# A fused attention and two-layer kernel: the first layer's gate as a tanh, a padding tile in its own pool, and a re-ordered list of steps for the first stage

## Chip, core and metric

The kernel runs on one core of a Trainium2 chip. The metric is the device time of one execution in microseconds; the profiled execution is one such run, recorded instruction by instruction. The engines are named as in the profile: PE is the matrix engine (PEld its weight loads), DVE the vector engine, ACT the scalar engine, POOL the GpSimd engine, and SP issues the transfers.

## What is computed

Three parts follow each other: attention with a feature map for 4 batches of 8 heads (576 positions, head size 64), a gated layer pair of 512 to 2048 to 512 for 2304 tokens, and a sum over four experts of 512 to 1024 to 512.

```python
def phi(x):
    proj = np.einsum('bhsd,df->bhsf', x, w_phi)
    proj = proj - np.max(np.abs(proj), axis=-1, keepdims=True)
    return np.concatenate([np.exp(proj), np.exp(-proj)], axis=-1)
...
num = np.einsum('bhsf,bhfd->bhsd', q_p, np.einsum('bhsf,bhsd->bhfd', k_p, v))
den = np.einsum('bhsf,bhf->bhs', q_p, np.sum(k_p, axis=2))[..., None] + 1e-06
...
h = x @ w_in
g = h * (1.0 / (1.0 + np.exp(-1.702 * h)))
x = g @ w_out
...
for e in range(E):
    h = np.maximum(x @ w1[e], 0.0)
    out += p[:, e:e + 1] * (h @ w2[e])
```

The weights `w_in` and `w_out` arrive as 64-bit floats, the rest as 32-bit floats.

## The kernel before, in words

The tokens are cut in two groups of 1024 and 1280, and each layer's hidden width in units of two 128-wide blocks: units 0 to 7 are the first layer on the first group, 8 to 15 the same layer on the second group, 16 to 47 the experts. A product of 32-bit values is made of three passes over a rounded high part (copied by ACT) and a low part (a subtraction, L208, on POOL or DVE).

The first stage holds the attention of 16 pairs of heads and, woven into it, units 0 to 6 of the first layer. There every step is a word of one long list, `ORDER`, and `in_order` ties each instruction to the one before it on its engine, so that the list fixes the order on PE, DVE, ACT, POOL and SP. A word such as `3.kn0` is a step of head pair 3; `q`, `k`, `v`, `n`, `t` are its matrix products, `kn`, `kp`, `en`, `ep` the exponentials of keys and queries (L591, L594, L549, L552). `h5.abs` and its like turn half a block of 64-bit weights into 32 bits: `abs` (L286), `rb` (L288) and `sg` (L290) on ACT, `cl` and `sh` (L292, L294) on DVE or POOL, `ad` and `mu` after them. In words of the layer, `F` is the first product (`plain_first`, L790), `Va` the sigmoid (L909), `Vb` its product with the hidden value (L912), `Ha` and `Hb` the high and low part, `S` the second product (`plain_second`, L825) and `E` its addition into `xa` (L834).

Unit 7 comes after the list, in `plain_unit`, with the second products of unit 6 between its own, and the preparation of unit 8 (`prep_sums`, `prep_in`, and the operands `xo` that `build_x` makes by subtractions on DVE, L389) goes beside it as background. From unit 8 on every unit is a `strassen_unit` of seven products per quarter (L733), and the second products of the unit before stand between them.

Before the first transfer lands, PE runs seven products of a zero tile (`warm`, L203). `norm_probs` (L434 to L437) scales the expert weights on DVE; it is outside the list, and the compiler places it.

Of the kernel before, what the change touches and what calls it, by code (L numbers as in the profile page):

```python
# [18 lines left out]
P = 128  # L19
# [23 lines left out]
EDGE = 120  # L43
NU = 7
# [28 lines left out]
h2.cl:1 0.v1 0.ve@0 2.k1@n5 1.ldv 2.k0@w1 1.rd1 h3.ld 2.qx1@1 2.qm0@1 3.ldk@1 3.qe1 1.kn0 0.ep 0.n0@w0 0.n1 4.ldq@1
5.ldq@0 2.kx1@0 2.ks1@0 2.kx0@0 1.kp1 1.rd2 2.qm1 1.kp0 2.ks0@0 2.r@n4 2.rm@0 2.ldv h2.sg 1.v0@n5 h2.sh 2.rd1 3.qx1@0
h3.abs 2.kn0 h3.sg 0.n2 0.fa@0 5.q0@w1 5.qx0@1 h2.rb@1 1.v1 1.ve@1 2.kp0 2.kn1 3.qm1 3.k0@w3 2.kp1 3.r@n4 1.es:0 1.en
2.v0@n5 0.fr 5.qe0@0 3.kx0@1 h2.ad:1 0.fm@0 4.ldk@0 3.rm@1 5.q1@w0 5.qe1 wl0.0:0 5.qm0@1 3.k1@n4 3.kx1@1 2.v1 1.ep
0.t1@w1 0.t0 2.ve@0 h3.rb@0 0.fh:0 3.ks0@1 2.rd2 3.kn0 3.ldv h2.mu:0 3.rd1 5.qx1@0 3.ks1@1 3.kp0 2.es:0 5.qm1 h3.cl:1
h4.ld h4.abs 4.q1@w3 4.k1@n5 4.q0@w0 4.qx0@1 4.qx1@0 1.n0@w1 1.n1 1.n2 h4.cl:1 4.qm0@0 4.qm1 4.kx1@0 5.ldk@1 5.k1@n4
5.kx1@1 8.ldq@0 4.qe0@2 4.qe1 1.fa@1 5.ks1@0 3.rd2 3.kn1 3.kp1 3.es:0 5.k0@w0 1.fr 5.r@n6 2.en 2.ep 4.ldv 5.kn1 h3.sh
5.rm@0 6.ldq@1 4.r@n7 4.rm@1 6.ldk@1 3.v0@n4 3.v1 3.ve@1 5.kx0@0 5.ks0@0 4.rd1 4.rd2 4.k0@w3 4.kx0@1 3.en 3.ep 2.n0@w0  # L80
2.n1 h4.rb@1 4.ks1@1 4.kn1 4.kp1 5.kn0 1.fm@1 4.ks0@1 4.kn0 5.rd1 2.n2 1.t1@w2 6.q0@w1 2.fa@0 6.qx0@1 1.t0 3.n0@w3
3.n1 1.fh:1 6.qe0@3 2.fr 2.fm@0 3.n2 3.fa@1 5.ldv 4.kp0 5.kp1 6.q1@w2 6.qx1@0 7.ldk@0 6.k0@w1 h3.ad:1 h3.mu:0 wl0.1:0
5.kp0 7.ldq@1 h5.ld 4.es:0 4.v0@n0 4.v1 xh0 xl0:0 5.rd2 6.kx0@0 6.qe1 3.fr 3.fm@1 4.en 4.ep 4.ve@0 h5.abs 5.v0@n1 5.v1
6.qm0@1 6.ks0@1 6.kn0 6.kp0 h5.sg 6.qm1 6.k1@n6 6.kx1@1 6.ks1@1 3.t1@w2 6.r@n7 6.rm@1 3.t0 3.fh:1 2.t1@w1 7.k1@n0 2.t0
2.fh:1 7.k0@w3 6.kn1 6.kp1 5.es:0 4.n0@w2 h4.sh 5.en 7.kx0@1 h4.ad:1 5.ep 6.ldv 4.n1 5.ve@1 4.n2 h5.cl:1 6.v0@n2 6.rd1
4.fa@0 7.kx1@0 6.v1 h4.sg 6.ve@0 8.ldk h4.mu:0 4.fr 4.fm@1 xh3 7.ks1@0 7.kn1 7.q1@w2 7.ks0@0 4.t1@w0 4.t0 4.fh:0
7.q0@w1 7.qx1@1 7.qx0@0 7.qm0@0 7.qm1 7.qe0@1 6.rd2 7.qe1 5.n0@w3 5.n1 5.n2 xl3:0 h5.rb@0 8.q0@w0 8.qe0@0 8.q1@w1 st0
7.r@n4 h5.sh 8.qe1 7.rm@0 h6.ld h6.abs 6.es:0 5.fa@1 5.fr 6.en 6.ep 5.fm@0 h6.sg 7.rd1 7.rd2 h5.ad:0 h5.mu:1 h6.cl:1
h7.ld h7.sg wi1 wl1.0:0 F0.0.0@n5 Va0.0.0@0 5.t1@w3 5.t0 5.fh:1 F0.1.0@n4 7.kp1 8.qx0@0 8.k1@n6 8.qx1@1 8.qm0@1 8.qm1
# [61 lines left out]
def fused(ctx: ExitStack, tc: tile.TileContext, qT, kT, v, w_phi, wg1, wg2, probs, out):  # L151
# [855 lines left out]
    def plain_unit(unit):  # L1007
        for n, (i, k, tag, behind) in enumerate(PLAIN):
# [5 lines left out]
            if n:  # L1014
                build_next()
# [78 lines left out]
```

## Time and profile before

| what | value |
|---|---|
| runs | 1333.04, 1338.75, 1336.97 us, median 1336.97 |
| profiled execution | 1336.96 us, span of its records 1335.2 us |
| PE busy | 1304.4 us, 98% of the span |
| DVE, POOL, ACT busy | 774.8, 679.8, 571.9 us (58%, 51%, 43%) |
| first product of unit 8 starts at | 345.41 us |

Busy is the time in which an engine had an instruction at work. PE is busy nearly always, so the table alone says little: what matters is in which stretches PE waits, for whom, and at which granted clock it works. [...]

### The profile page before, as it was taken

The page shows a single profiled execution, that of the slowest core. Times are in us where ns is not written, and L with a number is a line of the kernel's source. Part 1 is how long each engine was busy: PE and PEld are TensorE (multiplying, and loading weights), DVE is VectorE, ACT ScalarE, POOL GpSimd, SP SyncE. Part 2 cuts the span into 40 slices and gives each one's busy share as a digit, 9 for nine tenths or more (in the row PEclk, how much of TensorE's full clock was granted, in tenths as well). Part 3 has the DMA queues.
Part 4 walks back from the last instruction along what each step waited for, and adds up shares of the span by engine and source line. Part 5 has one row for each costly group of instructions (what it writes and reads, how often), then busy time and mean ns, then how long its engine had stood idle before and what let it go on. Part 6 is the DMA issues. An engine that isn't in the chain of part 4 may idle for free.

```text
span 1335.2 us, 19948 instructions
## 1 busy us (share of the span) xinstructions
PE 1304.4 (98%) x8231; PEld 1068.7 (80%) x8231; DVE 774.8 (58%) x1111; ACT 571.9 (43%) x824; POOL 679.8 (51%) x480
## 2 busy tenths in 40 slices
PE   7999999988999999999999999899999999999998
PEld 5877777777788888888888888778888888888887
DVE  7877768767834447654545545775455445445445
ACT  6889888775453334523323223243223222222310
POOL 4774656446956656855354463537324423443320
PEclk8999999989999999999999999999999999999999
DMA  7654434441100101011011110113001100110102
GB/s 219 202 169 142 149 122 158 143 146 64 64 32 32 63 33 32 32 64 64 32 64 61 34 64 32 63 32 127 32 32 36 60 32 32 56 40 32 32 0 79
DMA packets 45708, 96.87 MB, mean 73 GB/s; under 512 B 22706, under 2 KB 22834, under 8 KB 43570
## 3 DMA queue, kind: packets, MB, share of 16 engines
q1 hardware_dynamic: 45618, 95.61, 22.1%
q8 instruction: 64, 1.05, 0.3%
q14 instruction: 26, 0.21, 0.1%
HBM read 82.42 MB, written 13.18 MB: 72 GB/s over the span
## 4 chain that ended last, share of the span: by engine, by line
PE 88%; DVE 5%; ACT 4%; issue 1%; DMA 1%; POOL 0%; SPq 0%; DVEq 0%; ACTq 0%; POOLq 0%
PE psa L864 29%; PE psa L733 28%; PE psa L862 8%; PE psa L790 5%; PE psa L813 5%; PE psa L825 5%; PE psa L624 2%; PE psa L606 2%; DMA raws<-in_wg_dram 1%; PE psa L561 1%; PE psa L500 1%; ACT L909 1%; DVE xt L389 1%; PE psa L599 1%; DVE raws L389 1%
## 5 line engine op out<-in xcount | busy, mean ns | idle before, releaser
L733 PE MATMUL psa<-xo,win 128*128 128x512 f32 x1680 | 426.2, 392 | 1.0 <-DVE hs L740 0.9
L864 PE MATMUL psa<-wout,g 128*128 128x512 f32 x1536 | 387.8, 394 | 3.5 <-DVE xa L884 3.5
L733 PEld LDWEIGHTS psa<-xo,win 128*128 128x128 f32 x1680 | 315.0, 188 | 71.7 <-DVE hs L740 1.3
L864 PEld LDWEIGHTS psa<-wout,g 128*128 128x128 f32 x1536 | 286.8, 188 | 68.0 <-DVE xa L884 3.9
L208 POOL TENSOR_TENSOR wout<-raw,wout 128x1024 fp32r<-128x1024 f32 (+1 forms) x53 | 116.6, 2203 | 386.5 <-ACT wout L335 377.2
L884 DVE SCALAR_TENSOR_TENSOR xa<-psa,pn,xa 128x512 f32<-128x512 f32 x198 | 148.4, 749 | 144.2 <-PE psa L864 143.7
L711 ACT ACTIVATE g<-psa 128x512 fp32r<-128x512 f32 x96 | 57.5, 599 | 395.8 <-DVE psa L740 276.4
L208 POOL TENSOR_TENSOR g<-sg,g 128x512 fp32r<-128x512 f32 x59 | 79.4, 1350 | 93.8 <-ACT g L707 60.3
L712 DVE SCALAR_TENSOR_TENSOR g<-psa,g 128x512 fp32r<-128x512 f32 x96 | 66.4, 691 | 94.3 <-ACT g L711 94.3
L208 POOL TENSOR_TENSOR win<-raw,win 128x1024 fp32r<-128x1024 f32 (+1 forms) x51 | 113.9, 2236 | 11.0 <-ACT win L349 11.0
L208 POOL TENSOR_TENSOR win<-ss,win 128x1024 fp32r<-128x1024 f32 x40 | 98.0, 2450 | 9.5 <-ACT win L327 9.4
L825 PE MATMUL psa<-g,wout 128*128 128x512 f32 x384 | 99.0, 401 | 2.7 <-POOL g L208 0.7
L790 PE MATMUL psa<-xo,win 128*128 128x512 f32 x384 | 96.3, 400 | 2.8 <-DVE xa L834 2.1
L862 PE MATMUL psa<-g,wout 128*128 128x512 f32 x384 | 96.7, 394 | 0.0
L740 DVE TENSOR_TENSOR uu<-psa,mm 128x512 f32<-128x512 f32 x80 | 55.2, 690 | 64.0 <-PE psa L733 64.0
L825 PEld LDWEIGHTS psa<-g,wout 128*128 128x128 f32 x384 | 69.8, 188 | 22.4 <-issue 2.1
L790 PEld LDWEIGHTS psa<-xo,win 128*128 128x128 f32 x384 | 71.0, 190 | 20.5 <-DVE xa L834 2.9
L862 PEld LDWEIGHTS psa<-g,wout 128*128 128x128 f32 x384 | 71.2, 188 | 15.4
L813 PEld LDWEIGHTS psa<-xr,win 128*128 128x128 f32 x576 | 75.2, 189 | 4.0
L813 PE MATMUL psa<-xr,win 128*128 128x256 f32 x576 | 76.2, 281 | 0.0
L316 POOL TENSOR_TENSOR ss<-raw 128x256 f32<-128x256 f32 x80 | 61.9, 774 | 14.3 <-DMA raw<-in_wg_dram 9.0
L876 DVE TENSOR_TENSOR xa<-psa,xa 128x512 f32<-128x512 f32 x49 | 33.7, 689 | 35.2 <-PE psa L862 35.1
(126 smaller groups left out, 1700.9 us busy)
## 6 DMA issues: line engine op xcount, KB each, us to landing
raw<-in_wg_dram SPq DMA_DIRECT2D x32, 1024.0 KB
raws<-in_wg_dram SPq DMA_DIRECT2D x32, 512.0 KB
w_d<-raw SPq DMA_DIRECT2D x8, 1024.0 KB
raw<-w_d SPq DMA_DIRECT2D x8, 1024.0 KB
qraw<-in_qT_dram SPq DMA_DIRECT2D x16, 288.0 KB
kraw<-in_kT_dram SPq DMA_DIRECT2D x16, 288.0 KB
xa<-mx_d SPq DMA_DIRECT2D x8, 576.0 KB
mb<-mx_d SPq DMA_DIRECT2D x8, 576.0 KB
```

What stands on the lines that cost most here:

```text
L208: eng.tensor_tensor(out=dst, in0=src, in1=hi.bitcast(F32), op=ALU.subtract)
L316: nc.gpsimd.tensor_tensor(out=ss[:, n], in0=x0, in1=x1, op=op)
L711: nc.scalar.activation(out=hi, in_=src, func=AF.Relu)
L712: nc.vector.scalar_tensor_tensor(out=lo, in0=src, scalar=0.0, in1=hi.bitcast(F32), op0=ALU.max, op1=ALU.subtract)
L733: nc.tensor.matmul(ps, win[self.u][:, a, w, kc * P:(kc + 1) * P], xo[i][:, e, kc, :], start=start and k_ == 0, stop=stop and k_ == 5, skip ...
L740: nc.vector.tensor_tensor(out=out, in0=ps, in1=other, op=ALU.add)
L790: nc.tensor.matmul(ps, win[self.u][:, a, 2 * i + kc // 2, (kc % 2) * P:(kc % 2 + 1) * P], x[:, e, kc % 2, :], start=(n == 0), stop=(n == 11),)
L813: nc.tensor.matmul(ps, win[self.u][:, a, 2 * i + kc // 2, (kc % 2) * P:(kc % 2 + 1) * P], xo["rest"][e][:, kc, :], start=(k_ == 0), stop=( ...
L825: nc.tensor.matmul(ps, wout[self.u][:, a, i, t * P:(t + 1) * P], self.g[i, k][:, e, :], start=(n == 0), stop=(n == 5))
L862: nc.tensor.matmul(p, w[:, a, i, t_ * P:(t_ + 1) * P], v_, **f)
L864: nc.tensor.matmul(p, v_[:, t_ * P:(t_ + 1) * P], w[:, a, i, :], **f)
L884: nc.vector.scalar_tensor_tensor(out=o, in0=ps, scalar=col, in1=o, op0=ALU.mult, op1=ALU.add)
```

## The change

The gate h·sigmoid(1.702h) is computed as h·(1 + tanh(0.851h)), which is twice as large, and the conversion of `w_out` from 64 bits makes it half as large by other constants in the same two instructions. The padding tile `edge` is allocated in a pool of its own. The list is a new one: it now holds unit 7 and the preparation of unit 8 too (words `D`, `ld`, `ss`, `pi`, `px`), and one step `w3` with three more products of the zero tile; `plain_unit` and `PLAIN` are gone.

```diff
-NU = 7
+NU = 8
...
 ORDER = """
-0.ldq@0 0.q1@w0 h1.ld h1.abs h1.rb@0 0.qx1@0 0.ldk@0 h0.ld h0.abs 1.ldq@1 0.q0@w1 0.qx0@1 0.qm0@0 0.qm1 h1.cl:1
+0.ldq@0 0.q0@w0 0.qx0@0 0.q1@w1 0.qx1@1 h0.ld h0.abs h0.sg 1.ldq@1 w3@n6 1.q0@w2 h1.ld 1.q1@w3 0.qe0@0 0.qm0@0 0.qm1
...
+    edge = ctx.enter_context(tc.tile_pool(name="edge", bufs=1, side="right"))
+    edge.tile([P, EDGE], F32, name="edge")
     right = ctx.enter_context(tc.tile_pool(name="right", bufs=1, side="right"))
-    right.tile([P, EDGE], F32, name="edge")
...
         elif k == "rb":
-            nc.scalar.activation(out=rb[s], in_=l.bitcast(U32), func=AF.Copy, scale=2.0 ** -51, bias=2.0)
+            nc.scalar.activation(
+                out=rb[s], in_=l.bitcast(U32), func=AF.Copy, scale=2.0 ** (-51 - q // 2), bias=2.0 - q // 2
+            )
...
-            eng.tensor_scalar(out=m, in0=m, scalar1=W_MIN, scalar2=W_MAX, op0=ALU.max, op1=ALU.min)
+            eng.tensor_scalar(
+                out=m, in0=m, scalar1=W_MIN * (1 + q // 2 / 8), scalar2=W_MAX, op0=ALU.max, op1=ALU.min
+            )
...
+    def gate(out, src):
+
+        nc.scalar.activation(out=out, in_=src, func=AF.Tanh, scale=0.851)
+
+    def gated(t, src):
+        nc.vector.scalar_tensor_tensor(out=t, in0=t, scalar=1.0, in1=src, op0=ALU.add, op1=ALU.mult)
...
-                nc.scalar.activation(out=sg, in_=src, func=AF.Sigmoid, scale=1.702)
-                nc.vector.tensor_tensor(out=sg, in0=src, in1=sg, op=ALU.mult)
+                gate(sg, src)
+                gated(sg, src)
...
-                nc.scalar.activation(out=unit.sg[i, j], in_=src, func=AF.Sigmoid, scale=1.702)
+                gate(unit.sg[i, j], src)
...
-                nc.vector.tensor_tensor(out=sg, in0=src, in1=sg, op=ALU.mult)
+                gated(sg, src)
...
+        if name[0] == "w" and name[1].isdigit():
+            warm(int(name[1:]), int(slot[1:]))
...
+        elif name == "D":
+            third_area()
+        elif name[:2] in made:
+            next(made[name[:2]])
+        elif name[:2] == "px":
+            next(bx["023".index(name[2])])
...
-        (plain_unit if plain(u) else strassen_unit)(unit)
+        strassen_unit(unit)
```

How the new list moves instructions is shown at three places. The first is ACT, early in the stage, where the first gates of the layer stand between the exponentials of head pairs (`ek` of keys, `eq` of queries). ACT_TABLE_LOAD brings in the table of a function. Before:

```order
L349 CAST win_1073<-raw_134 128x1024
L909 ACT_TABLE_LOAD
L909 ACTIVATE sg_95<-psa 128x512
L594 ACT_TABLE_LOAD
L594 ACTIVATE ek_111<-ek_111 128x128
L349 CAST wout_89<-raw_133 128x1024
L909 ACT_TABLE_LOAD
L909 ACTIVATE sg_96<-psa 128x512
L591 ACT_TABLE_LOAD
L591 ACTIVATE ek_110<-ek_110 128x1024
L365 CAST xo_1187<-xa_71 128x1024
L594 ACTIVATE ek_110<-ek_110 128x1024
```

The same place in the new list, where L701 is the tanh and L593, L596, L551, L554 the exponentials:

```order
L593 ACTIVATE ek_113<-ek_113 128x1024
L514 COPY eq_111<-psa 128x2x288
L284 ACTIVATE raw_137<-raws_1_88 128x512
L596 ACTIVATE ek_113<-ek_113 128x1024
L701 ACTIVATE sg_98<-psa 128x512
L286 ACTIVATE xt_89<-raws_0_87 128x512
L286 ACTIVATE xt_90<-raws_1_88 128x512
L551 ACTIVATE eq_112<-eq_112 128x1152
L701 ACTIVATE sg_99<-psa 128x512
L919 CAST g_93<-sg_98 128x512
L554 ACTIVATE eq_112<-eq_112 128x1152
L671 COPY xa_74<-psa 128x448
```

No load stands between gates and exponentials any more; the built program has 42 loads on ACT before and one, its first instruction, now. The second place is DVE at the start, from the first large key subtraction (`ek` from psa and `mx`) of pair 0 on. Before:

```order
L586 TENSOR_TENSOR ek_110<-psa,mx_118 128x1024
L521 TENSOR_REDUCE r_115<-mb_107 128x2x9 x2
L518 STREAM_TRANSPOSE mb_107<-psa 128x576
L434 TENSOR_REDUCE psum_p<-pn 128x18
L435 TENSOR_SCALAR psum_p<-psum_p 128x18
L436 RECIPROCAL psum_p<-psum_p 128x18
L437 TENSOR_TENSOR pn<-pn,psum_p 128x72
L531 TENSOR_REDUCE m_117<-psa 36x32
L518 STREAM_TRANSPOSE mb_107<-psa 128x576
```

And now:

```order
L588 TENSOR_TENSOR ek_113<-psa,mx_121 128x1024
L520 STREAM_TRANSPOSE mb_110<-psa 128x576
L581 TENSOR_REDUCE mx_123<-psa 128x1
L533 TENSOR_REDUCE m_120<-psa 36x32
L588 TENSOR_TENSOR ek_114<-psa,mx_123 128x128
L581 TENSOR_REDUCE mx_124<-psa 128x1
L523 TENSOR_REDUCE r_117<-mb_110 128x2x9
L588 TENSOR_TENSOR ek_134<-psa,mx_124 128x128
L520 STREAM_TRANSPOSE mb_110<-psa 128x576 x2
```

The four instructions of `norm_probs` have left this place; they stand some 40 rows later. The third place is DVE at the end of the stage, where the subtractions of `build_x` (into `xt` and `raws`) are made. Before:

```order
L834 TENSOR_TENSOR xa_71<-psa,xa_71 128x512
L389 TENSOR_TENSOR xt_87<-xa_72 128x512 x2
L389 TENSOR_TENSOR xt_86<-xt_87,xa_72 128x512 x2
L389 TENSOR_TENSOR raws_0_84<-xa_72,xt_86 128x512 x2
L389 TENSOR_TENSOR raws_1_85<-xa_72 128x512
L834 TENSOR_TENSOR xa_71<-psa,xa_71 128x512 x2
L389 TENSOR_TENSOR raws_1_85<-xa_72 128x512
L834 TENSOR_TENSOR xa_71<-psa,xa_71 128x512 x2
```

And now, where L391 are the subtractions, L838 the additions into `xa`, L704 the gate's product and L300 a step of a weight's conversion:

```order
L391 TENSOR_TENSOR xt_90<-xa_75 128x512 x2
L300 SCALAR_TENSOR_TENSOR raw_137<-raws_0_87,raw_137 128x512
L704 SCALAR_TENSOR_TENSOR sg_98<-sg_98,psa 128x512
L704 SCALAR_TENSOR_TENSOR sg_99<-sg_99,psa 128x512
L838 TENSOR_TENSOR xa_74<-psa,xa_74 128x512
L391 TENSOR_TENSOR xt_89<-xt_90,xa_75 128x512 x2
L391 TENSOR_TENSOR raws_0_87<-xa_75,xt_89 128x512 x2
L838 TENSOR_TENSOR xa_74<-psa,xa_74 128x512 x3
```

The eight subtractions, seven of them in one piece before, are now broken into pieces of two, four and two, with gates and additions between.

## Rows read from the trace of the kernel before

**Rows 1.** The page: span and busy times of PE and PEld.

```profile
span 1335.2 us, 19948 instructions
...
PE 1304.4 (98%) x8231; PEld 1068.7 (80%) x8231; DVE 774.8 (58%) x1111; ACT 571.9 (43%) x824; POOL 679.8 (51%) x480
```

**Rows 2.** Stretches: length, then busy time by engine, granted PE clock, DMA share, GB/s.

```profile
0.00:345.40 345.40, 323.73 (x3623) 255.50 (x3624) 258.88 (x385) 272.72 (x381) 207.30 (x147) 0.97 0.48 149
0.00:40.00 40.00, 30.86 (x413) 22.18 (x415) 30.20 (x49) 26.28 (x41) 22.45 (x29) 0.91 0.73 213
40.00:345.40 305.40, 292.86 (x3218) 233.31 (x3213) 228.68 (x337) 246.44 (x341) 184.85 (x119) 0.98 0.44 141
```

**Rows 3.** Shorter stretches of the same view, where the granted clock was half.

```profile
13.80:20.70 6.90, 5.63 (x21) 2.39 (x21) 6.80 (x10) 5.46 (x10) 6.74 (x5) 0.51 0.77 243
...
92.40:95.70 3.30, 3.30 (x60) 3.30 (x62) 3.17 (x5) 3.11 (x4) 2.83 (x3) 0.50 0.02 3
...
181.10:184.40 3.30, 3.30 (x52) 3.18 (x48) 0.45 (x2) 1.25 (x3) 2.57 (x2) 0.50 0.36 114
...
293.80:300.50 6.70, 5.91 (x76) 5.47 (x77) 3.64 (x8) 5.12 (x8) 1.30 (x1) 0.50 0.51 151
```

**Rows 4.** Groups by line: the first and last of six groups of table loads.

```profile
L909 ACT ACT_TABLE_LOAD x21 | 26.9, 1283 | 2.5 <-PE psa L790 2.2
...
L286 ACT ACT_TABLE_LOAD x1 | 1.3, 1283 | 0.7 <-PEq L1080 0.7
```

**Rows 5.** Timeline of PE: its three longest waits after 40 us, in brackets.

```profile
92.28 1.97 PE L606 MATMUL psa<-v,ek 128*64 128x65 f32 x32 [1.80 <-ACT ek L594]
...
180.15 2.95 PE L624 MATMUL psa<-kv,eq 128*64 128x65 f32 x64 [2.31 <-ACT eq L552]
...
294.60 4.17 PE L624 MATMUL psa<-kv,eq 128*64 128x65 f32 x72 [3.13 <-ACT kv L613]
```

**Rows 6.** Timeline of ACT ahead of those three waits.

```profile
87.98 1.28 ACT L591 ACT_TABLE_LOAD   x1
...
91.17 1.05 ACT L594 ACTIVATE ek<-ek 128x1024 f32<-128x1024 f32 x1
...
177.64 1.28 ACT L552 ACT_TABLE_LOAD   x1
...
291.82 1.28 ACT L552 ACT_TABLE_LOAD   x1
```

**Rows 7.** Timeline of PE at the end of the stage.

```profile
319.92 0.73 PE L825 MATMUL psa<-g,wout 128*128 128x512 f32 x2 [0.71 <-ACT g L915]
321.38 2.56 PE L825 MATMUL psa<-g,wout 128*128 128x512 f32 x10 [0.73 <-POOL g L208]
326.04 5.76 PE L790 MATMUL psa<-xo,win 128*128 128x512 f32 x24 [2.10 <-DVE xa L834]
...
345.41 1.54 PE L733 MATMUL psa<-xo,win 128*128 128x512 f32 x6
```

**Rows 8.** Timeline of DVE at the end of the stage.

```profile
317.46 2.74 DVE L389 TENSOR_TENSOR xt<-xa 128x512 f32<-128x512 f32 x2
...
325.31 1.28 DVE L834 TENSOR_TENSOR xa<-psa,xa 128x512 f32<-128x512 f32 x2
```

**Rows 9.** Timeline of DVE and PE in the start.

```profile
18.95 2.30 DVE L437 TENSOR_TENSOR pn<-pn,psum_p 128x72 f32<-128x72 f32 x1
...
22.20 1.16 PE L561 MATMUL psa<-w_st,kraw 64*128 64x128 f32 x16 [1.49 <-DVE mb L518]
```

**Rows 10.** Groups by line: a fused DVE instruction, the gate's two, zero products.

```profile
L712 DVE SCALAR_TENSOR_TENSOR g<-psa,g 128x512 fp32r<-128x512 f32 x96 | 66.4, 691 | 94.3 <-ACT g L711 94.3
...
L912 DVE TENSOR_TENSOR sg<-psa,sg 128x512 f32<-128x512 f32 x28 | 19.2, 686 | 19.7 <-ACT sg L909 19.5
...
L909 ACT ACTIVATE sg<-psa 128x512 f32<-128x512 f32 x28 | 16.8, 598 | 6.2 <-PE psa L790 4.1 <-DVE g L208 1.6 <-POOL g L208 0.3
...
L203 PE MATMUL psa<-zero 128*128 128x512 f32 x7 | 3.4, 652 | 1.4 <-DVE zero L199 1.4
```

More of the change, by code (lines that the diff above doesn't have):

```diff
@@ L73 @@
[L73 to L77, printed above, removed]
@@ L147 @@
+S6.0.0@n7 E6.0.0 px2.1 ol7.1:0 E6.1.2 Ha7.0.1@2 Hb7.0.1:1 F7.1.1@n6 S6.0.3@n4 pi8.2 pi8.3 Va7.1.1@0 Vb7.1.1 Ha7.1.1@1
+px2.2 px3.1 ah1.0 ah1.1 px3.2 E6.0.3 Hb7.1.1:0 ld9 E6.1.0
 """
@@ L199, in fused, with warm @@
     nc.vector.memset(zero[:, 0, 0, :].bitcast(F32), 0.0)
-    def warm(n):
+    def warm(n, b=0):
         for _ in range(n):
-            nc.tensor.matmul(bank(0), zero[:, 0, 0, 0:P], zero[:, 0, 0, :], start=True, stop=True)
+            nc.tensor.matmul(bank(b), zero[:, 0, 0, 0:P], zero[:, 0, 0, :], start=True, stop=True)
     warm(WARM)
@@ L794, in plain_first @@
                     n += 1
-        def plain_value(self, i, k, ps):
-            older, self.stages = self.stages, deque()
-            self.value(i, k, ps)
-            self.finish(older)
         def finish(self, stages):
@@ L920, in fused @@
     pairs = [Pair(i) for i in range(B * NP)]
-    ready = build_x(1)
+    bx = build_x(1)
+    made = {"ss": prep_sums(NU), "pi": prep_in(NU)}
     def step(word):
@@ L938, in step @@
             pump(pre)
+        elif name == "D":
[4 more added lines that the diff above has]
+            next(bx["023".index(name[2])])
+        elif name[:2] == "ld":
+            next(load(int(name[2:])))
         elif name[:2] in ("xh", "xl"):
@@ L954, in fused @@
         in_order(lambda: step(word))
-    third_area()
+    for _ in range(3):
+        bx.popleft()
     norm_probs()
@@ L958, in fused @@
     ring["g"] = deque([g for g in gs if not any(g is x for x in held)] + held)
-    bg.append(load(NU + 1))
     before = units[NU - 1]
@@ L1005, in build_next @@
             free.append(bx.popleft())
-    def plain_unit(unit):
-        for n, (i, k, tag, behind) in enumerate(PLAIN):
-            ps = bank(TAGS.index(tag))
-            unit.plain_first(i, k, ps)
-            background(1)
-            seconds(*behind, paced=True)
-            unit.plain_value(i, k, ps)
-            if n:
-                build_next()
     def strassen_unit(unit):
@@ L1032, in fused @@
             bx = ready
-        if u + 1 < len(UNITS) and not plain(u + 1):
+        if u + 1 < len(UNITS):
             bg.append(prep_sums(u + 1))
```

161 lines of the change are left out of this document (81 added, 80 removed).

## Prediction

> **What bounds the kernel now.** I read the page first. PE is busy for 1304.4 of 1335.2 us [rows 1], so a gain can only come from time in which PE waits or works slowly. Next I read the view by stretches. The first stage, up to the first product of unit 8 at 345.41 us, has 323.73 us of busy PE [rows 2, 7], so 345.40 − 323.73 = 21.7 us of the kernel's 30.8 us of idle PE lie in it. Of these, 40.00 − 30.86 = 9.1 us fall into the first 40 us and 305.40 − 292.86 = 12.5 us into the rest [rows 2]. The reader should see here that ACT, the second busiest engine of the stage, is at work for 272.72 us of 345.40, and for 246.44 us of the 305.40 us after the start [rows 2]: 81% against 75% on DVE.
>
> The granted clock adds a second loss. [...] The last three follow the three longest waits of PE after the start: it waited 1.80 us up to 92.28, 2.31 us up to 180.15 and 3.13 us up to 294.60 [rows 5], and the clock was at 0.50 from 92.4, 181.1 and 293.8 on [rows 3].
>
> The view of the waits says who ended these three: an exponential of keys, one of queries, and the copy `kv` that stands behind one of queries [rows 5]. ACT's own timeline shows table loads in front of each: the loads at 87.98, 177.64 and 291.82 us are the last of four, four and three within the 13 us before, at 1.28 us each [rows 6]. So it is a queue on ACT, and not the data, that was late there.
>
> **The change part by part.** *Table loads.* Before, there are 42 loads, in six groups of which the largest is the 21 ahead of the sigmoid, at 1283 ns each [rows 4]. In the new program ACT has one. ACT is given back 41 × 1.283 = 52.6 us, so that 272.72 − 52.6 = 220 us are left in the stage. What of this reaches PE is read from the waits: in front of each of the three, the loads sum to 5.1, 5.1 and 3.8 us, more than the wait itself. I take all three waits off: 1.80 + 2.31 + 3.13 = **7.24 us**. The bounds are 0, if the same exponentials are late for another reason, and 7.24. Most other loads lie beside work of PE and are worth nothing; their cover is the products that PE has queued, and where a new order has less queued, one load would have cost at most its 1.28 us.
>
> *Clock.* In the three stretches PE was busy for 3.30 + 3.30 + 5.91 = 12.51 us at half speed [rows 3]. The same work at full speed is half of it: **6.25 us** back, provided that the waits go. Bounds: 0 and 6.25.
>
> *The end of the stage.* PE waits 0.71, 0.73 and 2.10 us there [rows 7]; the last was ended by an addition into `xa` that stood on DVE behind seven subtractions of `build_x`, one piece from 317.46 to 325.31 us [rows 8]. The new list breaks that piece up and puts gates and additions between. I take the three waits off: **3.54 us**, with 0 as the other bound. What is late next there is the operand `xo` of unit 8: the same subtractions end later when they yield to the gates, and they had some 20 us of PE's products as cover before (326.04 to 345.41). If that cover is short, PE waits at the first products of unit 8.
>
> *The start.* `norm_probs` held DVE for 2.30 us with its last instruction, and a transpose behind it ended a 1.49 us wait of PE [rows 9]. The four instructions now stand after the first pairs. I take **1.5 us**. Bounds: 0, and 9.1 + 2.8 = 11.9 us if all idle time of the start went, 5.63 / 2 = 2.8 us of which is the slow clock from 13.8 to 20.7 [rows 2, 3]; I take the low end since the first transfers and the chain from them to the first exponentials stay. Three more zero products cost about 3.4 / 7 = 0.5 us each, 1.5 us together [rows 10]. They stand between the queries of pair 0 and those of pair 1, where PE has no other work before DVE's and ACT's answers; I cost them at nothing, and at 1.5 us without that cover.
>
> *The gate itself.* No row shows a tanh. The sigmoid of 128x512 took 598 ns [rows 10], and ACT's instructions of that shape are within some tens of ns of it whatever they compute; I take the same. The fused instruction on DVE, 691 ns where it reads the matrix result beside an on-chip tile, stands against 686 ns for the plain product [rows 10]: 80 of them come to 80 × 5 ns = 0.4 us, off the path. The factor of one half rides on immediates of instructions that were there already, and the tile `edge` is never written or read: nothing.
>
> *What the new order adds.* The list changes the place of nearly every instruction of the stage, so new waits are sure to come. Their bounds are 0 and several of the kind seen. I take one of 2.10 us, like the longest that let the clock stand [rows 7].
>
> **Sum.** 7.24 + 6.25 + 3.54 + 1.5 − 2.1 = 16.4 us. The profiled execution took 1336.96 us, against a median of 1336.97, so the forecast for the median is 1336.96 − 16.4 = **1320.5 us**. Everything from unit 8 on keeps its order and its durations. A limit from above: after the start the stage can give back at most 12.5 + 6.25 = 18.8 us, so most of the forecast is that the stage becomes nearly free of waits.
>
> **The rivals.** *The waits stay, only their cause is renamed.* ACT had 73 us of idle time in the stage even with the loads, so an exponential may be late because DVE's maximum or a transfer was late. For this speaks that the largest of the three was a copy of `kv`, two instructions behind the exponential; against it, that ACT ran without a gap ahead of the first two. Only the end and the start would then gain, 3.54 + 1.5 = 5.0 us: 1332 us.
>
> *Slower.* In the new list PE waits for an engine that its order has put too late, and each such wait is paid twice, by itself and by the clock after it. By the middle one of the three this is 2.31 + 3.30 / 2 = 4.0 us. The place would be the change from unit 7 to unit 8, where DVE must finish the subtractions, low parts and additions in the time of PE's last products, or the first pairs, where the order is quite another one. Five such waits eat up 18.5 us of gains; to be slower by 0.5% takes 25.2 / 4.0, so more than six, and it gives 1343 us or more. Three in 300 us is what the trace of before shows, with ACT far fuller.
>
> *The clock holds through the start too.* It fell at 13.8 us after a stretch in which PE had little to do, and was back at 20.7 us [rows 3]. Three more zero products just ahead of that place could keep it up: 2.8 us more, 1317.7 us. [...] I leave this out of the likeliest sum.
>
> *More than the sum.* The stage loses all waits after 40 us and half of the start's 11.9 us: 18.8 + 6 = 24.8 us, 1312 us.
>
> **How the numbers follow.** The measurement of this kernel can tell about 0.5%, 6.7 us, from no change: faster means below 1330.3 us, slower above 1343.6 us. I give the forecast with its terms 0.50, the clock through the start 0.17, more than the sum 0.18, the renamed waits 0.10, and the slower list 0.05. The first three are faster, 0.85; the renamed waits are the same, 0.10. The range reaches down to 1310 us, which is the last gain with 2 us to spare, and up to 1331 us, which is the forecast with the 3.54 and the 1.5 us lost and about 5 us more of new waits; I leave out about 0.07 below and 0.12 above.
>
> **What would show it.** In the profile of the changed kernel ACT should have one table load, and ACT's busy time up to the first product of unit 8 should be near 220 us. That product should start near 329 us instead of 345.41. The clock should not be at half speed after 40 us, and no wait of PE for an exponential should exceed 1 us. The addition into `xa` should end no wait at the end of the stage, and the first products of unit 8 should follow without a wait for `xo` or for low parts of unit 7's weights. From unit 8 on, stretches should have their old lengths. The forecast is wrong if a wait of 2 us or more stands in the new stage with a fall of the clock behind it, if DVE, now the fullest engine after PE, ends such waits, or if the start takes longer since its key products come later.

## The result and the profile after

The changed kernel takes 1313.97 us (median of 4 runs, 1312.72 to 1314.64) beside 1336.65 us for the kernel before: a ratio of 0.9832 [0.9809, 0.9855], 22.7 us less. The forecast was 16.4 us less. The sign came as written, and the first stage to within 2.5 us, but two amounts that the sum does not contain, one in each direction, are as large as its biggest terms. The page of the changed kernel, beside [rows 1]:

```profile
span 1312.2 us, 19912 instructions
PE 1283.3 (98%) x8234; PEld 1070.4 (82%) x8234; DVE 780.5 (59%) x1117; ACT 516.7 (39%) x784; POOL 672.9 (51%) x472
```

Table loads in the view of groups, beside [rows 4]: one is left of 42, and it is the first instruction of ACT.

```profile
L284 ACT ACT_TABLE_LOAD x1 | 1.3, 1283 | 0.7 <-PEq L1085 0.7
```

The view by stretches, with the columns of [rows 2]; the granted clock is a share of full speed. The first product of unit 8 (L742, the L733 of before) starts at 326.53 us; unit 8 ends where unit 9's first product starts, at 360.39 us.

```profile
0.00:326.53 326.53, 313.45 (x3627) 255.89 (x3627) 256.18 (x383) 216.42 (x339) 191.87 (x135) 0.98 0.49 155
0.00:40.00 40.00, 34.78 (x529) 26.33 (x531) 31.92 (x54) 29.08 (x46) 20.30 (x26) 1.00 0.77 226
40.00:326.53 286.53, 278.67 (x3100) 229.56 (x3100) 224.25 (x329) 187.34 (x294) 171.57 (x109) 0.98 0.45 145
326.53:360.39 33.86, 26.80 (x115) 20.78 (x114) 31.27 (x34) 13.81 (x21) 30.15 (x19) 0.90 0.18 62
360.39:1312.20 951.81, 943.03 (x4495) 793.69 (x4493) 493.09 (x701) 286.44 (x425) 450.89 (x320) 1.00 0.13 46
```

The last two stretches of the kernel before, in the same view:

```profile
345.41:370.63 25.22, 24.48 (x115) 19.68 (x114) 21.70 (x26) 12.51 (x19) 21.28 (x14) 1.00 0.13 43
370.63:1335.20 964.57, 956.23 (x4495) 793.53 (x4493) 494.16 (x701) 286.62 (x425) 451.27 (x320) 1.00 0.14 46
```

Read as three parts, the 23.0 us between the profiled spans are −18.88 up to unit 8, +8.64 in unit 8, and −12.76 from unit 9 on. The last part is the surprise: the same 4495 products, with idle time of 8.78 us against 8.34, and yet PE's busy time is 13.2 us less. PE does not wait less there. About 1 us of the 12.76 lies in unit 30, where the second group of tokens of the experts is prepared: the clock was at half there for 6.8 us in the kernel before and for 3.4 us in the changed one. The view by stretches, before and then after:

```profile
849.13:876.14 27.01, 23.53 (x91) 18.64 (x90) 21.27 (x23) 5.85 (x8) 12.48 (x7) 0.87 0.12 39
832.71:858.73 26.02, 22.30 (x91) 18.00 (x90) 21.19 (x23) 5.84 (x8) 12.59 (x7) 0.93 0.12 41
```

In the other units the products themselves follow each other more closely: in the experts' first group the second products of odd units start 227 ns apart in the median, where they had 234 (table below). Unit 8 is the opposite: 7.06 us of idle PE where there were 0.74, and a granted clock of 0.90.

The waits of PE between 40 us and unit 8, by what was waited for: us in total, times, longest.

```profile
PE psa L563 <- DVE ek L588: 3.0, 1, 3.0
PE psa L569 <- DMA kraw<-in_kT_dram: 2.3, 1, 2.3
PE psa L658 <- DVE on L641: 2.1, 2, 1.9
```

The three waits behind ACT of [rows 5] are gone. Three others have come: for DVE up to 46.87 us, for DVE again up to 100.31 and for a transfer up to 183.17. The view by stretches has half a clock behind each, as in [rows 3]:

```profile
46.80:50.20 3.40, 3.33 (x38) 3.10 (x40) 3.23 (x6) 2.80 (x5) 1.37 (x1) 0.51 0.38 83
101.40:104.80 3.40, 3.40 (x70) 3.40 (x66) 0.62 (x2) 2.77 (x5) 0.31 (x1) 0.50 0.53 148
183.30:186.70 3.40, 3.40 (x12) 2.03 (x13) 1.55 (x4) 1.94 (x5) 2.79 (x2) 0.50 0.03 5
```

**Unit 8.** PE's timeline at the change of units, beside [rows 7] (L742 are unit 8's first products, L829 second products of unit 7):

```profile
326.53 1.07 PE L742 MATMUL psa<-xo,win 128*128 128x512 f32 x4
327.92 0.73 PE L742 MATMUL psa<-xo,win 128*128 128x512 f32 x2 [0.33 <-DVE xo L206]
332.96 4.37 PE L829 MATMUL psa<-g,wout 128*128 128x512 f32 x10 [4.30 <-DVE sg L704]
338.72 1.63 PE L742 MATMUL psa<-xo,win 128*128 128x512 f32 x6 [1.39 <-DVE xa L838]
```

The 4.30 us were ended by a gate's product on DVE (L704), because that product is the last reader of the accumulation bank that PE wants next. DVE's timeline shows what stood ahead of it; L206 is the low part of a split, L391 the subtractions of `build_x`, L838 the additions:

```profile
328.39 1.17 DVE L206 TENSOR_TENSOR xo<-xt,xo 128x512 fp32r<-128x512 f32 x1
329.48 0.68 DVE L838 TENSOR_TENSOR xa<-psa,xa 128x512 f32<-128x512 f32 x1
330.08 2.23 DVE L206 TENSOR_TENSOR g<-sg,g 128x512 fp32r<-128x512 f32 x1
332.23 0.67 DVE L704 SCALAR_TENSOR_TENSOR sg<-sg,psa 128x512 f32<-128x512 f32 x1
332.83 1.15 DVE L206 TENSOR_TENSOR xo<-xt,xo 128x512 fp32r<-128x512 f32 x1
333.91 3.47 DVE L391 TENSOR_TENSOR raws<-xa 128x512 f32<-128x512 f32 x2
337.30 1.87 DVE L838 TENSOR_TENSOR xa<-psa,xa 128x512 f32<-128x512 f32 x3
```

DVE has no gap here, and its instructions of one shape differ widely: an addition that reads one operand from the matrix result takes 0.68 us, while a subtraction of two on-chip tiles takes 1.15, 1.17 or 2.23 us. POOL's timeline beside it:

```profile
328.97 2.79 POOL L206 TENSOR_TENSOR win<-ss,win 128x1024 fp32r<-128x1024 f32 x1
331.72 3.41 POOL L206 TENSOR_TENSOR xo<-xa,xo 128x512 fp32r<-128x512 f32 x2
```

The 2.23 us instruction started at 330.08, inside POOL's instruction, which ended at 331.76, and ended 0.55 us after it. Over the whole changed kernel such instructions on two on-chip tiles took 1.22 us in the median where a POOL instruction overlapped them and 0.68 us where none did (numbers in the last section), and the additions from the matrix result 0.68 us in both cases. So in this trace the ones held up stand beside POOL; why, no run shows. PE's granted clock then stood at 0.50 from 330.1 to 336.9 us.

### The profile page after: what moved, and what is told of

It reads as the page before. It is cut to its first block, busy times and chain, and to the rows that moved or that the text cites. A ratio compares the mean times of both kernels' runs of the same rounds, so it can differ in the third digit from the quotient of the medians.

```text
span 1312.2 us, 19912 instructions
## 1 busy us (share of the span) xinstructions
PE 1283.3 (98%) x8234; PEld 1070.4 (82%) x8234; DVE 780.5 (59%) x1117; ACT 516.7 (39%) x784; POOL 672.9 (51%) x472
## 4 chain that ended last, share of the span: by engine, by line
PE 89%; DVE 6%; DMA 3%; POOL 1%; issue 1%; ACT 0%; SPq 0%; DVEq 0%; ACTq 0%
PE psa L868 29%; PE psa L742 28%; PE psa L866 8%; PE psa L829 6%; PE psa L799 6%; PE psa L817 5%; PE psa L626 2%; PE psa L608 1%; DMA xa<-mx_d 1%; DVE xo L206 1%; PE psa L502 1%; PE psa L563 1%; POOL eq L548 1%; DVE raws L391 1%; DMA kraw<-in_kT_dram 1%
## 5 line engine op out<-in xcount | busy, mean ns | idle before, releaser
L742 PE MATMUL psa<-xo,win 128*128 128x512 f32 x1680 | 421.5, 390 | 3.0 <-DVE xa L838 1.4
L868 PE MATMUL psa<-wout,g 128*128 128x512 f32 x1536 | 381.3, 391 | 3.7 <-DVE xa L888 3.7
L742 PEld LDWEIGHTS psa<-xo,win 128*128 128x128 f32 x1680 | 314.4, 188 | 69.3 <-ACT win L329 1.8
L206 POOL TENSOR_TENSOR wout<-raw,wout 128x1024 fp32r<-128x1024 f32 (+1 forms) x51 | 113.9, 2235 | 372.6 <-ACT wout L337 369.5
L206 POOL TENSOR_TENSOR g<-sg,g 128x512 fp32r<-128x512 f32 x56 | 77.3, 1381 | 96.2 <-ACT g L716 59.3
L206 POOL TENSOR_TENSOR win<-raw,win 128x1024 fp32r<-128x1024 f32 (+1 forms) x52 | 115.5, 2224 | 5.6 <-ACT win L351 3.0
L206 POOL TENSOR_TENSOR win<-ss,win 128x1024 fp32r<-128x1024 f32 x40 | 98.3, 2457 | 8.3 <-ACT win L329 8.2
L829 PE MATMUL psa<-g,wout 128*128 128x512 f32 x384 | 96.7, 401 | 5.2 <-DVE sg L704 4.3
L866 PE MATMUL psa<-g,wout 128*128 128x512 f32 x384 | 95.3, 390 | 0.0
L799 PE MATMUL psa<-xo,win 128*128 128x512 f32 x384 | 92.4, 392 | 0.4 <-POOL win L206 0.2
L829 PEld LDWEIGHTS psa<-g,wout 128*128 128x128 f32 x384 | 73.1, 193 | 23.3 <-DVE sg L704 4.7
L799 PEld LDWEIGHTS psa<-xo,win 128*128 128x128 f32 x384 | 71.5, 188 | 17.2 <-POOL win L206 0.7
L866 PEld LDWEIGHTS psa<-g,wout 128*128 128x128 f32 x384 | 71.1, 188 | 14.4 <-DVE xa L880 0.2
L701 ACT ACTIVATE sg<-psa 128x512 f32<-128x512 f32 (+1 forms) x72 | 39.3, 548 | 84.8 <-DVE psa L749 32.5
```

The source lines that it names most:

```text
L206: eng.tensor_tensor(out=dst, in0=src, in1=hi.bitcast(F32), op=ALU.subtract)
L742: nc.tensor.matmul(ps, win[self.u][:, a, w, kc * P:(kc + 1) * P], xo[i][:, e, kc, :], start=start and k_ == 0, stop=stop and k_ == 5, skip ...
L799: nc.tensor.matmul(ps, win[self.u][:, a, 2 * i + kc // 2, (kc % 2) * P:(kc % 2 + 1) * P], x[:, e, kc % 2, :], start=(n == 0), stop=(n == 11),)
L829: nc.tensor.matmul(ps, wout[self.u][:, a, i, t * P:(t + 1) * P], self.g[i, k][:, e, :], start=(n == 0), stop=(n == 5))
L866: nc.tensor.matmul(p, w[:, a, i, t_ * P:(t_ + 1) * P], v_, **f)
L868: nc.tensor.matmul(p, v_[:, t_ * P:(t_ + 1) * P], w[:, a, i, :], **f)
```

## The experiments

All times are set beside runs of the kernel before on the same chip (medians 1334.0 to 1337.9 us). "First" is the start of unit 8's first product in the profile, "unit 8" its length. The moved addresses of the later experiments and the kernel without the filler were executed once each; their unit lengths and the spacing of their products tell more than their times.

### What each part is worth

**The gate alone**: the kernel before, its old list and old padding, with the tanh and the halved `w_out`. One of the two places of the gate; the constants of the conversion are those of the change:

```diff
-                nc.scalar.activation(out=sg, in_=src, func=AF.Sigmoid, scale=1.702)
-                nc.vector.tensor_tensor(out=sg, in0=src, in1=sg, op=ALU.mult)
+                nc.scalar.activation(out=sg, in_=src, func=AF.Tanh, scale=0.851)
+                nc.vector.scalar_tensor_tensor(out=sg, in0=sg, scalar=1.0, in1=src, op0=ALU.add, op1=ALU.mult)
```

> The kernel before (old list, padding in the common pool) with only the tanh gate and the halved w_out: one table load. By the prediction's first two terms the three waits of 1.80, 2.31 and 3.13 us and the slow clock behind them go, 13.5 us: about 1323 us. Rival, that those exponentials were late for another reason or that the old list puts its waits elsewhere: 1333 to 1337 us.

Measured: 1319.67 us (1317.61 to 1321.45), ratio 0.9877 [0.9861, 0.9894]. First at 328.56 us, 16.85 earlier than before; unit 8 25.17 us, as before. All that is left of PE's waits between 40 us and unit 8, in the view of waits:

```profile
PE psa L825 <- POOL g L208: 1.1, 1, 1.1
PE psa L790 <- DVE xa L834: 0.9, 1, 0.9
PE psa L825 <- ACT g L915: 0.7, 1, 0.7
```

The clock is at full speed from 40 us to unit 8, beside the third line of [rows 2]:

```profile
40.00:328.56 288.56, 285.82 (x3227) 228.40 (x3223) 225.09 (x337) 192.51 (x300) 184.62 (x119) 1.00 0.47 149
```

The tanh takes as long as the sigmoid did, 596 against 598 ns [rows 10]. So the loads caused the three long waits and the slow clock behind them, the last three of the four stretches of [rows 3], in the old order. The gain is some 3 us more than expected.

**The loads back**: the changed kernel, with its new list and pool, and the sigmoid and the whole `w_out` again (42 loads).

```diff
-        nc.scalar.activation(out=out, in_=src, func=AF.Tanh, scale=0.851)
+        nc.scalar.activation(out=out, in_=src, func=AF.Sigmoid, scale=1.702)
```

> The changed kernel (new list, padding in its own pool) with the sigmoid and the full w_out again, so that ACT has its 42 table loads. If the loads are what the stage gained by, its waits for exponentials come back: 10 to 16 us more than the changed kernel, 1324 to 1330 us. Rival, that the new order would hide them: 1314 to 1317 us.

Measured: 1332.91 us (1326.48 to 1336.28), ratio 0.9971 [0.9954, 0.9989]. First at 345.71, unit 8 34.93 us. The waits for ACT are back, in other places:

```profile
PE psa L626 <- ACT eq L554: 6.4, 2, 5.2
PE psa L563 <- DVE ek L588: 3.7, 1, 3.7
PE psa L626 <- ACT xa L671: 3.0, 1, 3.0
```

The loads cost 18.9 us under the new list (1332.91 − 1313.97), some 3 us more than the expectation's upper end, and 17.2 and 14.6 under the old one (without and with the padding moved; medians against the kernel before and against the padding alone, below). The rival of the renamed waits falls on both sides.

**The padding alone**: the kernel before with two lines moved.

```diff
+    edge = ctx.enter_context(tc.tile_pool(name="edge", bufs=1, side="right"))
+    edge.tile([P, EDGE], F32, name="edge")
     right = ctx.enter_context(tc.tile_pool(name="right", bufs=1, side="right"))
-    right.tile([P, EDGE], F32, name="edge")
```

> The kernel before with only the padding tile in its own pool; nothing else differs. Addresses: this moves the tiles wout0, g0 to g4 and sg0, sg1 by 480 bytes, from an address of 96 modulo 128 to one of 0 modulo 128. Theory A, the address of these operands sets the pace of the products: from unit 9 on the units take 26.24, 20.40 and 26.04 us as in the changed kernel, 12 us in sum, and the first stage gains about 2 us by its 720 products, so about 1322.5 us. Theory B, the quicker later units come from the gate or the list: no change, 1336.7 us.

Measured: 1323.83 us (1320.52 to 1326.97), ratio 0.9904 [0.9882, 0.9926]. First at 347.21 us, no earlier than before; unit 8 25.13; the units behind it have exactly the lengths of the changed kernel: 26.24 us (before 26.33 and 26.58 in turn), 20.40 (20.67 and 20.84), 26.04 (26.32 and 26.42). From unit 9 on, beside the second of the two stretches of the kernel before above:

```profile
372.34:1325.20 952.86, 944.06 (x4495) 794.40 (x4493) 493.22 (x701) 286.56 (x425) 450.91 (x320) 1.00 0.14 46
```

That is 11.7 us less than before, with unit 30 at 27.05 us as before. In this profile the first stage did not gain the 2 us that were expected of it.

**All but the padding**: the changed kernel with the tile back in `right`.

> The changed kernel with the padding tile back in the pool of the other tiles. Theory A: units from 9 on as slow as before (26.33 and 26.58, 20.67 and 20.84, 26.32 and 26.42 us), 12 us, and the first stage about 2 us longer: about 1328 us. Theory B: 1314 us.

Measured: 1325.04 us (1322.42 to 1326.55), ratio 0.9911 [0.9896, 0.9926]. First at 324.75, unit 8 33.73, and every later unit as long as before. A tile that nobody touches, moved by 480 bytes, is worth 10 to 13 us: 13.1 alone, 11.1 beside gate and new list, 10.5 beside the gate (with the next experiment).

### What the new list is worth

**The old list with gate and padding**: the kernel before with both edits above and nothing else.

> The kernel before with the tanh gate, the halved w_out and the padding tile in its own pool, and the old list: the whole change without the new list. If the parts add up (gate alone 17.2 us, padding alone 13.1 us in the first four runs), 1336.9 - 17.2 - 13.1 = 1306.6 us, so that the new list is worth a loss of some 7 us. Rival, that the new list is needed for what the gate gives back: 1314 us or more.

Measured: 1309.21 us (1307.18 to 1310.29), ratio 0.9790 [0.9776, 0.9804]. It beats both kernels, the changed one by 4.8 us. First at 329.32 us, 2.8 later than in the changed kernel, but unit 8 follows without the waits, as its timeline shows:

```profile
329.32 1.52 PE L734 MATMUL psa<-xo,win 128*128 128x512 f32 x6
330.68 1.52 PE L826 MATMUL psa<-g,wout 128*128 128x512 f32 x6
332.04 1.52 PE L734 MATMUL psa<-xo,win 128*128 128x512 f32 x6
333.40 1.52 PE L826 MATMUL psa<-g,wout 128*128 128x512 f32 x6
```

and in its view by stretches:

```profile
329.32:354.51 25.19, 24.15 (x116) 19.67 (x115) 21.82 (x26) 12.42 (x19) 21.29 (x14) 1.00 0.12 43
```

Without the padding's move the same holds: gate alone 1319.67, gate and new list 1325.04. The new list brings unit 8 forward by 2.8 to 3.8 us and makes it 8.6 to 8.7 us longer: it loses 5 us.

**The gate's product first**: the changed kernel with the list's last words put in another order. The low part `Hb7.0.1` goes behind both gates and the last addition, the subtractions `px2` behind the gates.

```diff
-... E6.0.0 px2.1 ol7.1:0 E6.1.2 Ha7.0.1@2 Hb7.0.1:1 F7.1.1@n6 ... Vb7.1.1 Ha7.1.1@1 px2.2 px3.1 ... ld9 E6.1.0
+... E6.0.0 ol7.1:0 E6.1.2 Ha7.0.1@2 F7.1.1@n6 ... Vb7.1.1 Ha7.1.1@1 px2.1 px2.2 E6.1.0 Hb7.0.1:1 px3.1 ... ld9
```

> The changed kernel with the last words of its list in another order: on DVE the last gate's product of unit 7 goes ahead of a low part of an operand of unit 8 and of a low part of unit 7, and the last addition of unit 6 ahead of unit 8's subtractions. Theory: the 4.30 us and 1.39 us waits at the first products of unit 8 come from the bank that this gate holds and the bank that this addition holds, both late on DVE. Then unit 8 takes 26 to 28 us in place of 33.9 us, the clock does not fall there, and the time is 1306 to 1309 us. Rival: DVE is full there, and the wait moves to the next operand: unit 8 at 31 us or more, 1311 to 1314 us.

Measured: 1313.03 us (1311.34 to 1314.66), ratio 0.9824 [0.9811, 0.9838]; unit 8 33.71 us. PE's timeline:

```profile
327.37 1.66 PE L829 MATMUL psa<-g,wout 128*128 128x512 f32 x6 [1.06 <-DVE sg L704]
331.98 2.88 PE L742 MATMUL psa<-xo,win 128*128 128x512 f32 x6 [2.95 <-DVE xa L838]
```

The wait for the gate falls from 4.30 to 1.06 us, one for an addition of 2.95 us stands behind it, and the clock falls to half from 332.0 to 335.4 us. The theory fell and the rival held: this order does not help. The likely reason is that DVE has too much to do there. In the changed kernel it is busy for 31.27 of unit 8's 33.86 us with 34 instructions, with the old list for 21.82 of 25.19 with 26: the new list does some 9 us of DVE's work behind the seam, the change from unit 7 to unit 8, that the old one did ahead of it, part of it as longer instructions beside POOL (1.15 to 2.23 us above, where such instructions took 0.68 us without POOL). No run moved that work alone.

### What the padding changed

The move of `edge` shifts `wout0`, the five `g` tiles and the two `sg` tiles by −480 bytes. In the changed kernel all operands of these products (`xo`, `win`, `wout0`, `wout1`, `g`) start at the same place modulo 2048 in their partition. Each experiment below is the changed kernel with other paddings, and the table gives the offset of a tile's start from that common place. Second products of even units read `wout0`, of odd units `wout1` (never moved). "Spacing" is the median time from one product's start to the next, within the second products of the experts' first group, worked out from the trace.

| kernel | wout0 | g | spacing, even units (wout0 with g) | spacing, odd units (wout1 with g) | time, us |
|---|---|---|---|---|---|
| before | +480 | +480 | 227 ns | 234 ns | 1336.65 |
| after | 0 | 0 | 227 ns | 227 ns | 1313.97 |
| e7_shift_64 | +64 | +64 | 230 ns | 235 ns | 1326.85 |
| e8_g_shift | 0 | +480 | 234 ns | 234 ns | 1327.51 |
| e9_wout_shift | +96 | +128 | 235 ns | 232 ns | 1330.29 |
| e11_shift_128 | +128 | +128 | 227 ns | 232 ns | 1321.71 |
| e11_shift_256 | +256 | +256 | 227 ns | 227 ns | 1312.32 |

The edit of e7_shift_64 (e11_shift_128 and e11_shift_256 have 32 and 64 in place of 16):

```diff
-    edge.tile([P, EDGE], F32, name="edge")
+    edge.tile([P, EDGE - 16], F32, name="edge")
     right = ctx.enter_context(tc.tile_pool(name="right", bufs=1, side="right"))
+    right.tile([P, 16], F32, name="shift")
```

> The changed kernel with wout0, g0 to g4, sg0 and sg1 moved by 64 bytes, to an address of 64 modulo 128; it was 0 in the changed kernel and 96 before. If what counts is the address modulo 64, the units are as quick as in the changed kernel (26.24, 20.40, 26.04 us; products 227 ns apart). If it is the address modulo 128, they are slower, as before, 10 to 12 us in sum.

> The changed kernel with `wout0`, the g and the sg tiles all 128 bytes further on (352 bytes of padding in the pool of its own, 128 in front of `wout0`), so that they stay at a multiple of 128 bytes, but not of 256. In the changed kernel all operands of the layer's products lie at the same place modulo 2048, so the multiple that counts may be any up to that. Theory (multiples of 128 count): units of 26.24, 20.40 and 26.04 us as in the changed kernel, 1314 us. Rival (a larger multiple counts; e9 had g at 128 past it and was slow in units whose operands were all at multiples of 128): units of 26.3 to 26.6, 20.7 to 20.9 and 26.3 to 26.5 us, 1325 to 1330 us.

> The same with 256 bytes (224 in the pool of its own, 256 in front of `wout0`). If multiples of 128 or of 256 count: units as in the changed kernel, 1314 us. If only multiples of 512 or more do: the longer units, 1325 to 1330 us.

At +64 and at +128 the units are longer (26.3 to 26.5, 20.5 to 20.9 us), at +256 they are those of the changed kernel to 0.01 us, but for those at a change of groups. So, of the places tried, multiples of 256 bytes are as good as the common place; my first theories, 64 and then 128, fell.

In e8_g_shift `edge` stands between `wout0` and the `g` tiles; in e9_wout_shift 96 bytes stand ahead of `wout0` and 32 behind it, which puts g at +128. I had taken that for the common place when I wrote the expectation, so the run does not test `wout0` alone. The edit of e8_g_shift, less the lines that take `edge`'s own pool away:

```diff
     wout0 = right.tile([P, 2, 2, 512], F32R, name="wout0")
+    right.tile([P, EDGE], F32, name="edge")
     gs = [right.tile([P, 2, HALF], F32R, name="g%d" % i) for i in range(5)]
```

> The changed kernel with g0 to g4, sg0 and sg1 at 96 modulo 128 and wout0 at 0. Before, even units (wout0 at 96) and odd ones (wout1 at 0) differed by 0.10 to 0.25 us. If the two operands of a product slow it when they differ, every unit is now like the slower ones of before (26.58, 20.84, 26.42 us), 16 us over the changed kernel by unit 47. If each misplaced operand costs by itself, all units lie between the changed kernel's and before's slower ones.

> The changed kernel with two paddings around the weights tile `wout0` alone: it lies at 96 past a multiple of 128 bytes, while g, sg and all others stay at 0. Theory (a product is slow when its two operands lie differently): the second products of even units, which read wout0 and run during odd units, start 234 ns apart, those of odd units 227 ns as in the changed kernel; odd units 9, 11 and so on then take about 26.5 instead of 26.24 us, and the time is 1319 to 1322 us. Rival (only the address of the moving operand g counts): 227 ns in both, 1314 us. Rival (any tile off the line slows all): both at 230 to 234 ns, 1327 us.

In e8_g_shift every unit is like the slower ones of before (26.57, 20.84, 26.41 us), the first of the two outcomes. In e9_wout_shift all units are longer than in the changed kernel (26.53 to 26.56, 20.80 to 20.91, 26.31 to 26.55).

In this stretch of all seven kernels a product whose two operands lie at different places modulo 256 bytes is spaced by 232 to 235 ns in the median, and one whose operands lie alike by 227 to 230. One timeline shows both kinds; e11_shift_128 at the change from an even unit's second products to an odd unit's, 12 products to a row (a row's own time reaches into the next row, since a product is recorded for 395 ns in the mean there, longer than its spacing):

```profile
619.70 2.89 PE L869 MATMUL psa<-wout,g 128*128 128x512 f32 x12
622.42 1.53 PE L743 MATMUL psa<-xo,win 128*128 128x512 f32 x6
...
636.17 2.96 PE L869 MATMUL psa<-wout,g 128*128 128x512 f32 x12
638.96 1.55 PE L743 MATMUL psa<-xo,win 128*128 128x512 f32 x6
```

12 products take 622.42 − 619.70 = 2.72 us where both operands are at +128, and 638.96 − 636.17 = 2.79 us where `wout1` is at 0 and g at +128.

This rule is not the whole effect. Where a tile is off the common place, products of operands that lie alike lose too: in the kernel before, those of `wout0` and g have the median of 227 ns, but a mean of 228.8 against 226.6 in the changed one. Summed from the starts of the products from unit 9 on, without units 30 to 32 and 47, second products take 388.8 us before and 382.1 after (6.7 less), and first products, neither of whose operands moved, 337.3 and 333.6 (3.7 less).

### What the filler products are worth

**Without the step `w3`**: the changed kernel less one word of the list.

```diff
-... 1.ldq@1 w3@n6 1.q0@w2 ...
+... 1.ldq@1 1.q0@w2 ...
```

> The changed kernel without the word `w3`, the three added products of the zero tile. Theory that they keep up the clock of the start: half a clock returns for some 7 us near 14 us and the first product of unit 8 comes about 3 us later than 326.53. Rival (they do nothing that can be told, since two kernels with them also fell to half clock near 17 us): the start is as in the changed kernel or has a short fall, and the first product of unit 8 comes within 1.7 us of 326.53.

Measured: 1312.76 us, first at 325.38 us. The clock of the start, in the view by stretches:

```profile
0.00:40.00 40.00, 31.94 (x522) 24.77 (x524) 32.96 (x54) 28.70 (x45) 20.31 (x26) 1.00 0.77 228
13.80:20.70 6.90, 5.14 (x90) 4.15 (x89) 6.90 (x13) 5.82 (x10) 3.95 (x3) 1.00 0.92 268
```

Without the filler the clock stayed up in this run, and in e7_shift_64, e8_g_shift and e9_wout_shift, three of the nine profiled kernels with the new list and the filler, it fell near 17 us. This is e9_wout_shift:

```profile
17.00:20.40 3.40, 3.40 (x24) 2.92 (x22) 2.82 (x7) 2.91 (x6) 2.22 (x2) 0.50 0.93 267
```

So the filler was neither enough to hold the clock nor needed for it, and it costs nothing that one run can show. The four profiled kernels with the old list all have half a clock for 6.8 or 10.2 us in the start.

## Why the prediction was right, and where its steps were off

**Table loads and clock (7.24 and 6.25 us): right.** One load is left, ACT is busy for 216.42 us up to unit 8 (220 forecast), and no wait for an exponential exceeds 1 us. In the gate alone, without the new list, unit 8 comes 16.85 us earlier, against 13.49 for these two terms. The rest of the 16.85 us comes with the end of the stage: the gate alone has waits of 1.1, 0.9 and 0.7 us there, in place of 0.71, 0.73 and 2.10 [rows 7] and smaller ones. The gate's own term is right too: 596 ns for the tanh, and 681 ns for its product on DVE in the changed kernel. For the tanh it took the sigmoid's time, since ACT's other instructions of that shape lay near it; in the kernel before their larger groups took 587 to 671 ns in the mean, the lowest a copy, the highest an absolute value:

```profile
L758 ACT COPY mm<-psa 128x512 f32<-128x512 f32 x40 | 23.5, 587 | 3.9 <-PE psa L733 2.0
...
L286 ACT ACTIVATE raw<-raws 128x512 f32<-128x512 f32 x32 | 21.5, 671 | 12.0 <-DMA raws<-in_wg_dram 12.0
```

**The end of the stage (3.54 us): the term is right in place and wrong in sign.** It was put down to the new list breaking up the `build_x` piece. The same paragraph named what is late next, "the operand `xo` of unit 8", and gave no price for it. The addition into `xa` still ends a wait, of 1.39 us inside unit 8, and the operand one of 0.33; the largest, 4.30 us, is for a bank that a gate's product on DVE had not yet freed, which the text did not see. With the half clock behind it the place costs 8.64 us. The three waits before unit 8 did go; they came back behind its first products, and larger.

**The start (1.5 us): too small.** In the first 40 us PE's idle time fell from 9.14 to 40.00 − 34.78 = 5.22 us, but 9.30 − 7.75 = 1.55 us of the difference are the three zero products, which do none of the kernel's work:

```profile
7.75 1.62 PE L201 MATMUL psa<-zero 128*128 128x512 f32 x3
9.30 1.24 PE L502 MATMUL psa<-qraw,w_st 64*128 64x288 f32 x8
```

The half clock of [rows 3], worth 2.8 us, did not come: 9.14 − 5.22 − 1.55 + 2.8 = 5.2 us in sum. This is the rival "the clock holds through the start too" (1317.7 us, chance 0.17), but not by its mechanism. It rested on three zero products, and in the one run without them the clock holds as well. That such products keep the clock up was the author's guess, from a fall behind a stretch in which PE was busy for 1.64 of 3.40 us (from 10.4 to 13.8 us). What kept the clock up no run shows: PE has 529 products in these 40 us where it had 413 [rows 2], since those of the next pairs come earlier, but in e9_wout_shift, where the clock fell, it has 521, and without the filler, where it held, 522.

**New waits (−2.1 us): mis-sized.** Three in the stage, 2.98, 2.27 and 1.91 us, with 3.33 + 3.40 + 3.40 = 10.13 us of work at half speed, half of which is lost: 12.2 us. The forecast counted one such wait, and without its clock; the price "paid twice" stood in the slower rival only. Unit 8 comes on top. The slower rival was right about the place, "the change from unit 7 to unit 8", and about DVE; it needed more than six such waits, and there were four. By its own signs the prediction was wrong about the new list: waits of 2 us or more with a fall of the clock behind them stand in the new stage, and DVE ends such waits.

**The stage as a whole: right, by parts that offset each other.** Its end was forecast near 329 us and came at 326.53. The new list gains in the start and loses in its own waits.

**"The tile `edge` is never written or read: nothing" and "Everything from unit 8 on keeps its order and its durations": these steps failed.** The order is kept; unit 8 is 8.64 us longer, and from unit 9 on 12.76 us are gained, all but about 1 us of them by the address of tiles that the tile `edge` moves. The text had looked at what uses `edge`, not at what lies behind it. Without this part the changed kernel takes 1325.0 us, and the sum would have been 4.5 us too low instead of 6.5 us too high: the two failed steps have opposite signs. That the total came so near to the forecast is in part luck: without the address's gain it would be 1325.0 us, and without unit 8's loss some 1305 us, below the range.

**"More than the sum" (1312 us, chance 0.18)** is nearest in time, and its mechanism, a stage without any wait after 40 us, did not come about.

What stays open: why products of `xo` and `win`, which did not move, are also spaced by 228 to 231 ns in most units of the slower kernels and by 227 in the changed one, about a third of what the address gives from unit 9 on; which part of the new order keeps the clock up in the start; and how the three new waits of the stage could be taken out of the list.

## What to carry to other kernels

Price an edit of a tile that nobody uses by what it moves: look up the start of every matrix operand behind it, and keep the operands of a long chain of products, those of the products woven between them too, at the same place modulo 256 bytes: the two kernels here that did so, the changed one and e11_shift_256, had all these products 227 ns apart in the median, and each of the other kernels in the table had some of them 230 to 235 ns apart. When a resource is relieved (ACT's loads here), first run the old order with it: a list searched anew can lose at its seam what it gains inside, and the seam, where the next stage's operands and the last stage's results meet on one engine, is the place to price. And count a wait of PE of some 2 us with the half clock behind it: in the stage and the seam of the two kernels those of 1.80 to 4.30 us had it, but for one of 2.10 us; in e2_no_pad_pool and e3_gate_first one of 1.9 us had not.

## What the runs showed of the hardware that was not expected

The spacing of 128x512 products depends on where their operands start in a partition: in the stretch of the table, in the median, 227 ns when both lie alike modulo 256 bytes at 0, +128, +256 or +480, 230 ns with both at +64, and 232 to 235 ns when they differ. With what the products between them gain, this is 10 to 13 us of 1337 here.

In the changed kernel 71 instructions of DVE subtract or add two on-chip tiles of 128x512. The 17 that no POOL instruction overlaps took 0.68 us in the median; the other 54 took 1.22 us in the median and up to 2.90. An addition with one operand from the matrix result took 0.68 us in both cases.
